# Decay rows in four loads on three queues, fillers on another bank, and the first half of w_in ahead of x0, in a state-space and GELU kernel

## The chip, the cores and the metric

The kernel runs on one core of a Trainium2 chip. A core has five engines that run their own instruction streams and meet at semaphores: TensorE (PE, matmuls, with a separate row PEld for loading weights), VectorE (DVE), ScalarE (ACT), GpSimd (POOL) and SyncE (SP). Data move between the chip's main memory (HBM), the on-chip SBUF and, by the engines alone, the matmul accumulators (PSUM, in banks of 128 x 512 fp32). Transfers are done by 16 DMA engines; SP, ACT and POOL each have a queue from which they issue them. The metric is the time of one execution on the device in microseconds; the median over several executions is compared.

## The reference

Two stages. The first is a state-space layer over 4 batches, 8 heads, 768 positions, head size 32 and state size 16, worked in chunks. In each chunk, with `cum` the running sum of the log of the clipped decays `a`:

```
L = exp(cum_i - cum_j), i >= j;   M = (C B^T) * L
y = M x  +  (C state) * exp(cum)
state = exp(sum) * state + sum_j B_j x_j exp(cum_end - cum_j)
```

The second takes `y` as 3072 tokens of 256 features, and computes `g = gelu_tanh(y w_in)` with 2048 hidden features, and `out = g w_out`. Inputs and output are fp32.

## The kernel before

The chunk is 128 positions, so a batch has 6 chunks and there are 24 in all. They are grouped in units: chunk 0, chunk 1, and then pairs, 13 units.

**Decay.** The decays of all 32 (batch, head) rows are loaded into one tile `a_t` of 128 x 256: four groups of 32 partitions, group q holding positions 192 q onward. Its first 192 columns come by one load on SP (line 153) and the other 64, for three groups, by one load on ACT (line 155); the rest is set to one by DVE (line 142). DVE clips it (`f_clip`, line 268), runs a product scan with restarts at chunk ends (`f_R`, 272), transposes the result in 32 x 32 blocks into `rt` (`f_RT`, 277) and takes reciprocals (`f_recip`, 281). C is scaled with the one and B with the other (`f_mul`, line 311), both to bf16. So the factor exp(cum_i - cum_j) sits in the operands, and M needs only the causal mask.

**One batch.** The scaled C and B are transposed by PE (`f_T`, 322) into PSUM and copied to SBUF as `ce` (C, in two copies with alternate heads zeroed by `par`) and `bh` (B); `f_N` (357) transposes `bh` back per chunk to `bn`. Batch 0 has its own split version of these steps (`sequence0`), in which B's transposes go to the bank `yb` and C's to `o_ps`; the copy of B is done by DVE for the first two chunks (257) and by ACT for the rest (253).

**One unit.** `f_G` (390): eight Gram matmuls per chunk pair into the four banks `gb`. `f_M` (400): DVE multiplies by the causal mask `tri`. `f_D` (411): the state's increment B^T x into a bank `hp`. `f_S` and `f_SP` (459, 461, 468): DVE updates the state and spreads it with `bmask`. `f_Y` (433, 442): PE adds the chunk's own part and the state's part into `yb`. `f_yev` (451): ACT copies the result to `xm`, transposed as the next stage wants it. x is cast to bf16 by POOL (255) ahead of that.

**Second stage.** `f_s1` (492): w_in times `xm` into `hp` or, for some groups of unit 0, `o_ps`; `f_gelu` (500) on ACT; `f_s2` (509): w_out; `f_oev` (516, 518) copies the result out and `f_store` (522) has SP issue the store. w_in comes in two halves of 1 MB (`load_wi`, 244) and w_out in four quarters (`load_wo`, 249); POOL casts them, and ACT half of the first quarter of w_in.

**The order.** All engines' programs are fixed when the kernel is built. Each step is a node with an engine, an estimated duration, its dependencies and a priority; `run_order` (line 31) simulates the engines with these estimates, picks at each time the node of the best priority that is ready, and writes the instructions in that order. Loads are nodes of a DMA engine with a duration and a delay `done` until they can be used; SP issues them in the order in which the nodes are made:

```
an = load(TD + 0.3, none)
load_bc_n(0, 1, 0)
load_x_n(0)
load_w_n(0)
load_x_n(1)
load_w_n(1)
```

Where PE would be idle early on by the planner's clock, `idle` (736) puts in filler matmuls on a tile of zeros `wz` (line 744), which write columns 384 to 511 of `yb` and are read by nobody. There are 69 of them, in blocks of 44, 7, 10, 6, 1 and 1. The number in a block is worked out from the length of the planner's gap. Every DMA has one of eight completion semaphores in turn, and a DMA whose semaphore has been used waits at its issuing engine until the earlier user is complete. The second pair of w_out quarters waits in addition until POOL has done the last w_in cast.

Of the kernel before, what the change touches and what calls it, by code (L numbers as in the profile page):

```python
# [93 lines left out]
def kernel(  # L94
# [10 lines left out]
    nc = tc.nc  # L105

    batch, H, S, D = x.shape
    N = B.shape[-1]
    Q = 128
# [3 lines left out]
    QS = S // 4  # L113
# [25 lines left out]


    a_t = const.tile([128, 2 * Q], FP32, name="a_t")
    nc.vector.memset(a_t[96:128, QS:], 1.0)
    XF, X16 = {}, {}
    U = [dict() for _ in range(batch)]

    def load_bc(b, i):
# [3 lines left out]
        nc.sync.dma_start(out=d["bc"][:, i],  # L150
                          in_=(B, C)[i][b].rearrange("h (p r) n -> p h (r n)", r=R6))

    nc.sync.dma_start(out=a_t[:, 0:QS], in_=bass.AP(
        tensor=a.tensor, offset=a.offset, ap=[[QS, 4], [S, batch * H], [1, QS]]))
    nc.scalar.dma_start(out=a_t[0:96, QS:], in_=bass.AP(
        tensor=a.tensor, offset=a.offset + QS,
        ap=[[QS, 3], [S, batch * H], [1, 2 * Q - QS]]))

    wz = const.tile([128, 512], BF16, name="wz")
    nc.vector.memset(wz, 0.0)  # L160
    warm = const.tile([128, 1], FP32, name="warm")
# [45 lines left out]
    for e in range(2):  # L207
        nc.vector.tensor_reduce(out=par[:, e:e + 1],
                                in_=bmp[:, e, :, 0:1].rearrange("p g o -> p (g o)"),
# [12 lines left out]
    gb = ps1.tile([128, 4, 512], FP32, name="gb")  # L222
    yb = ps1.tile([128, 512], FP32, name="yb")
# [252 lines left out]
    def third(u, i):  # L476
        return u < 1 and (4 * u + i) % 3 == 0
# [51 lines left out]
    def add(eng, dur, fn, *args, deps=(), prio=0.0, done=None):  # L529
        n = Node(eng, dur, (lambda: fn(*args)), deps, prio,  # L530
                 (0.26 if eng == "PE" else 0.0) if done is None else done)
        n.name = f"{fn.__name__}{args}"
        nodes.append(n)
        return n
# [7 lines left out]
    def load(dur, fn, *args, deps=()):  # L542
        nload[0] += 1
        return add("DMA", dur, fn, *args, deps=deps, done=0.9, prio=nload[0])
# [3 lines left out]
    Gn, Mn, Dn, Yn, yevn, Sn, SPn = ({} for _ in range(7))  # L548
    cen, bhn, bnn = {}, {}, {}

    an = load(TD + 0.3, none)

    def load_bc_n(b, *which):
        for i in which:
            bl[(b, i)] = load(1.6, load_bc, b, i)

    def load_x_n(*us):
        for u in us:
            xl[u] = load(0.87 * len(UNITS[u]), load_x, u)

    def load_w_n(*qs, o=False):
        for q in qs:
            if o:
                won_l[q] = load(1.5, load_wo, q)
            else:
                win_l[q] = load(2.5, load_wi, q)

    load_bc_n(0, 1, 0)
    load_x_n(0)
    load_w_n(0)  # L570
    load_x_n(1)
    load_w_n(1)
    load_x_n(2)
    load_w_n(0, 1, 2, 3, o=True)
# [14 lines left out]

    cl = add("DVE", 0.35, f_clip, deps=[an], prio=-90)  # L590
    R_ = add("DVE", 0.68, f_R, deps=[cl], prio=-89)
    RT_ = add("DVE", 0.27, f_RT, deps=[R_], prio=-88)
    rc1 = add("DVE", 0.46, f_recip, 0, 1, deps=[RT_], prio=-62)
    pen = add("DVE", 0.32, f_pe, deps=[R_], prio=-19)
    mul_c = add("DVE", 0.97, f_mul, 0, 1, deps=[bl[(0, 1)], rc1], prio=-61)
    mul_b = add("DVE", 0.97, f_mul, 0, 0, deps=[bl[(0, 0)], RT_], prio=-60)
    rc2 = add("DVE", 1.35, f_recip, 1, batch, deps=[RT_], prio=45)
    ppn = add("PE", 0.4, f_pp, deps=[pen], prio=-28)
    pendn = add("ACT", 0.2, f_pend, deps=[ppn], prio=-29)
    ppn.takes("hp", pendn)  # L600

    PB = 1000.0
    gpn, geln, oevn = {}, {}, {}

# [19 lines left out]
    def sequence0():  # L624

        t1 = add("PE", 0.34, f_T, 0, 1, deps=[mul_c], prio=-70)
        t0 = add("PE", 0.34, f_T, 0, 0, deps=[mul_b, t1], prio=-69)
        fa = [add("ACT", 0.4, f_F0, e, "ACT", 0, PA, deps=[t1], prio=-70) for e in range(2)]
        ea = add("DVE", 0.36, f_E, 0, 0, "DVE", 0, PA, deps=[t0], prio=-70)
        na = add("PE", 0.12, f_N, 0, 0, 2, deps=[ea], prio=-25)  # L630
        ba = add("ACT", 0.3, f_bn, 0, "ACT", 0, 2, deps=[na], prio=-20)
        fb = [add("ACT", 0.55, f_F0, 0, "ACT", PA, 128, deps=[t1], prio=-18),
              add("ACT", 0.55, f_F0, 1, "ACT", PA, 128, deps=[t1], prio=-17)]
        eb = add("ACT", 0.55, f_E, 0, 0, "ACT", PA, 128, deps=[t0], prio=-47)
        nb = add("PE", 0.24, f_N, 0, 2, CPB, deps=[eb, na], prio=-24)
        bb = add("ACT", 0.4, f_bn, 0, "ACT", 2, CPB, deps=[nb], prio=-19)
        t1.takes("o", *fa, *fb)
        t0.takes("yb", ea, eb)
        na.takes("hp", ba, bb)
        for c in range(CPB):  # L640
            cen[c], bhn[c], bnn[c] = (fa, ea, ba) if c < 2 else (fa + fb, eb, bb)


    for u, cs in enumerate(UNITS):
        n = len(cs)
        q = 10.0 * cs[0]
        e = "POOL"
        xcn[u] = add(e, 0.42 if n == 1 else 0.62, f_castx, u, e, deps=[xl[u], Yn.get(u - 5)], prio=q - 12)
        if u == 0:
            sequence0()  # L650
# [14 lines left out]
        for k in range(n):  # L665
# [3 lines left out]
            else:  # L669
                ms.append(add("DVE", 1.24, f_M, u, k, 0, 4, deps=[gn] + ms,  # L670
                              prio=q + 1 + 0.1 * k if u > 1 else -16 + 2 * u + 0.1 * k))
# [5 lines left out]
        for k, gc in enumerate(cs):  # L677
            if gc % CPB == CPB - 1:
# [4 lines left out]
                          prio=q + 1.5 + 0.1 * k if u > 1 else -13.5 + u)  # L683
        Dn[u].takes("hp", *ss)
        deps = ms + [xcn[u]] + [SPn[c - 1] for c in cs if c % CPB > 0]
# [11 lines left out]
    for u, cs in enumerate(UNITS):  # L697
        n = len(cs)
        c0 = cs[0]
        per = 512 // (n * Q)  # L700
        for i in range(4 * n):
            f_last = (i * per + per - 1) // 4
            gpn[(u, i)] = add("PE", 0.437, f_s1, u, i,
                              deps=[yevn[u]] + wi_n[f_last] + ([gpn[(u, i - 1)]] if i else [gpn.get((u - 1, 4 * len(UNITS[u - 1]) - 1))] if u > 2 else []),
                              prio=PB + 10 * c0)
            geln[(u, i)] = add("ACT", 0.57, f_gelu, u, i, deps=[gpn[(u, i)]], prio=PB + 10 * c0 + i)
            gpn[(u, i)].takes("o" if third(u, i) else "hp", geln[(u, i)])
    prev = None
    s2_first = []
    for u, cs in enumerate(UNITS):  # L710
        n = len(cs)
        per = 512 // (n * Q)
        for tt, gc in enumerate(cs):
            pool = "yb" if gc >= NCH - TAIL and gc % 2 == 0 else "o"
            oeng = "DVE" if gc >= NCH - TAIL and gc % 2 else "ACT"
            for q in range(4):
                need = [geln[(u, i)] for i in range(4 * n) if i * per <= 4 * q + 3]
                nd = add("PE", 0.437, f_s2, u, tt, q, pool, deps=need[-1:] + [wo_n[q], prev],
                         prio=PB + 45 + 10 * cs[0] + tt)
                if q == 0:  # L720
# [15 lines left out]
    def idle(t0, t1):  # L736
        t0 = max(t0, 1.25)
        n = int((t1 - t0 - 0.05) / (0.107 if t0 < 6.3 else 0.2 if 9.5 < t0 < 13.2 else 0.07))
        if gpn[(0, 0)].start is not None or n < 1:
            return None  # L740

        def fill():
            for _ in range(n):
                nc.tensor.matmul(out=yb[:, 384:512], lhsT=wz[:, 0:128], rhs=wz[:, 0:128],  # L744
                                 start=True, stop=True)
        return fill

    pools = {"hp": 2, "o": 1, "gram": 2, "yb": 1, "wf": 4, "ob": 6}
    for t, fn in run_order(nodes, pools, idle=idle, wait=("DVE", "POOL")):
        fn()  # L750
# [30 lines left out]
```

## Time and profile before

| | us |
|---|---|
| median of 13 executions | 124.94 (124.44 to 125.89) |
| profiled execution | 124.93 |
| its span, first to last instruction | 123.2 |
| PE busy | 111.4 (90%) |
| ACT busy | 75.2 (61%) |
| DVE busy | 63.3 (51%) |
| POOL busy | 19.7 (16%) |
| clip of the decays starts | 5.66 |
| first transposes (batch 0, C) start | 8.77 |
| first Gram products start | 13.52 |
| first w_in matmuls start | 17.30 |
| transposes of batch 1 start (C, B) | 30.52, 32.96 |

The span is what the profile covers; the 1.73 us between it and the execution's time lie before the first and after the last instruction. Times in the profile count from the start of the span. A view by timeline gives for each group of instructions its start, length, engine, source line, operation, and in brackets how long the engine had been idle and what released it. The chain of work that ended last is followed back from the last instruction; it names a DMA where a transfer was the last thing waited for, and SPq where SP's queue of DMA issues was. A view by windows gives the busy time of each engine in a stretch, the clock that was granted to TensorE (1.00 is full, 0.5 half), the mean busy share of the 16 DMA engines (over 1 where records of transfers overlap) and the bytes moved per second. Over the whole span the granted clock is 0.972; it is low between 9 and 16 us.

### The profile page before, as it was taken

Reading aid. Unit: us, or ns where it says so; the run is one execution under the profiler, and the core shown is the slowest. Engines: PE = TensorE matmul, PEld = TensorE weight load, DVE = VectorE, ACT = ScalarE, POOL = GpSimd, SP = SyncE. Lnnn points to the kernel's source line nnn. Section 1 sums busy time; section 2 is a strip of 40 time slices with the busy share of each in tenths; the row PEclk is TensorE's granted clock in tenths of the full one; section 3 lists DMA queues with packets and bytes.
Section 4 is the critical chain, followed back from the end, with each engine's and each line's share of the span. In section 5 each row is a group of like instructions: output and inputs, shape, how many; then the busy total and the mean of one; then the engine's idle time right before and its main releaser. Section 6 shows DMA issues by size and latency. Waiting matters only on the chain.

```text
span 123.2 us, 3421 instructions
## 1 busy us (share of the span) xinstructions
PE 111.4 (90%) x1471; PEld 94.5 (77%) x1471; DVE 63.3 (51%) x112; ACT 75.2 (61%) x145; POOL 19.7 (16%) x37
## 2 busy tenths in 40 slices
PE   5916987998699999999999999999999999999980
PEld 5915756785597788797878888787878888888870
DVE  5193399874837998753959618292936000000100
ACT  2206359574395676579667688656677778666410
POOL 7310666750211123121000000000000000000000
PEclk9995599999999999999999999999999999999999
DMA  0989998999959989980111010011110110011121
GB/s 16 250 203 243 367 213 249 337 211 170 167 103 286 170 143 284 169 150 11 37 43 43 5 43 20 28 43 43 48 43 0 48 43 21 24 48 43 43 85 43
DMA packets 39637, 13.96 MB, mean 113 GB/s; under 512 B 33863, under 2 KB 39111, under 8 KB 39623
## 3 DMA queue, kind: packets, MB, share of 16 engines
q1 hardware_dynamic: 39524, 13.73, 48.5%
q8 instruction: 11, 0.18, 0.7%
q10 hardware_dynamic: 99, 0.02, 0.1%
q14 instruction: 3, 0.02, 0.1%
HBM read 10.61 MB, written 3.15 MB: 112 GB/s over the span
## 4 chain that ended last, share of the span: by engine, by line
PE 70%; DMA 13%; SPq 8%; DVE 4%; POOL 2%; issue 1%; DVEq 0%
PE o_ps L509 29%; PE hp L492 29%; DMA wf<-in_moe_w_in_dram 8%; DMA bc_t<-in_C_dram 6%; SPq L236 4%; PE yb L509 3%; PE gb L390 2%; PE yb L433 2%; PE yb L442 2%; POOL w_in_sb L255 2%; PE gb L322 2%; DVE ch L257 1%; DVE bc L311 1%; SPq L244 1%; SPq L150 1%; PE gb L357 1%
## 5 line engine op out<-in xcount | busy, mean ns | idle before, releaser
L500 ACT ACTIVATE gT<-hp 128x512 bf16<-128x512 f32 x94 | 52.2, 596 | 20.1 <-PE hp L492 19.8
L492 PE MATMUL hp<-xm,w_in_sb 128*128 128x256 bf16 (+1 forms) x400 | 50.7, 266 | 0.3 <-ACT xm L451 0.2
L509 PE MATMUL o_ps<-w_out_sb,gT 128*128 128x256 bf16 x352 | 47.3, 273 | 0.0
L492 PEld LDWEIGHTS <-w_in_sb 128*128 128x128 bf16 x416 | 37.2, 98 | 5.8 <-issue 1.8
L509 PEld LDWEIGHTS <-gT 128*128 128x128 bf16 x384 | 37.1, 98 | 4.8 <-issue 0.4
L400 DVE TENSOR_TENSOR m<-gb,tri 128x1024 bf16<-128x1024 f32 (+1 forms) x25 | 29.0, 1174 | 2.6 <-PE gb L390 2.5
L518 DVE COPY o_sb<-o_ps 128x256 f32<-128x256 f32 x2 | 0.8, 424 | 25.1 <-PE o_ps L509 25.1
L255 POOL CAST x<-x_t 128x512 bf16<-128x512 f32 (+1 forms) x13 | 8.3, 639 | 29.5 <-DMA x_t<-in_x_dram 18.9
L468 DVE SCALAR_TENSOR_TENSOR sp_new<-s_new,pend,bmask 128x256 bf16<-128x256 f32 x20 | 11.0, 553 | 0.2
L744 PE MATMUL yb<-wz 128*128 128x128 bf16 x69 | 8.2, 305 | 2.6 <-DVE warm L162 1.4
L516 ACT ACTIVATE o_sb<-o_ps 128x256 f32<-128x256 f32 x20 | 7.7, 384 | 4.4 <-ACT gT L500 2.7
L461 DVE SCALAR_TENSOR_TENSOR s_new<-s_new,pend,hp 128x64 f32<-128x64 f32 x16 | 4.5, 280 | 10.3 <-PE hp L411 9.9
L744 PEld LDWEIGHTS <-wz 128*128 128x128 bf16 x69 | 7.3, 147 | 3.0 <-issue 1.5
L451 ACT ACTIVATE xm<-yb 128x512 bf16<-128x512 f32 (+1 forms) x13 | 7.4, 567 | 3.3 <-PE hp L411 3.0
L322 PEld LDWEIGHTS <-bc 128*128 128x128 bf16 x48 | 3.4, 104 | 5.3 <-DVE bc L311 4.0
L442 PE MATMUL yb<-m,x 128*32 128x128 bf16 x192 | 6.2, 220 | 0.0
L390 PE MATMUL gb<-ce,bh 32*128 32x256 bf16 x96 | 5.0, 283 | 1.1 <-DVE m L400 1.1
L339 ACT ACTIVATE ce<-o_ps,par 128x258 bf16<-128x258 bf16 (+1 forms) x4 | 2.2, 582 | 5.5 <-PE o_ps L322 5.5
L433 PE MATMUL yb<-ce,sp_new 128*32 128x128 bf16 x160 | 5.3, 221 | 0.0
L459 DVE COPY s_new<-hp 128x64 f32<-128x64 f32 x4 | 0.9, 222 | 8.5 <-PE hp L411 8.5
L311 DVE TENSOR_TENSOR bc<-bc_t,pt 128x768 bf16<-128x768 f32 x4 | 3.8, 954 | 2.5 <-DMA bc_t<-in_C_dram 2.5
L255 POOL CAST w_in_sb<-wf 128x1024 bf16<-128x1024 f32 (+1 forms) x4 | 3.8, 981 | 5.6 <-DMA wf<-in_moe_w_in_dram 5.6
(59 smaller groups left out, 61.4 us busy)
## 6 DMA issues: line engine op xcount, KB each, us to landing
x_t<-in_x_dram SPq DMA_DIRECT2D x24, 128.0 KB, 4.6
out_dram<-o_sb SPq DMA_DIRECT2D x24, 128.0 KB, 1.7
wf<-in_moe_w_in_dram SPq DMA_DIRECT2D x2, 1024.0 KB, 8.5
wf<-in_moe_w_out_dram SPq DMA_DIRECT2D x4, 512.0 KB, 5.8
bc_t<-in_C_dram SPq DMA_DIRECT2D x4, 384.0 KB, 4.7
bc_t<-in_B_dram SPq DMA_DIRECT2D x4, 384.0 KB, 4.6
a_t<-in_a_dram SPq DMA_DIRECT2D x1, 96.0 KB
a_t<-in_a_dram ACTq DMA_DIRECT2D x1, 24.0 KB
```

Source lines behind the costliest of these rows:

```text
L255: nc.gpsimd.tensor_copy(out=o, in_=i)
L390: nc.tensor.matmul(out=gb[:, g, 256 * k:256 * k + 256], lhsT=bh_of(gc)[32 * g:32 * g + 32], rhs=ce_of(gc)[32 * g:32 * g + 32], start=True, ...
L400: nc.vector.tensor_tensor(out=MT[gc][:, g0:g1], in0=gb[:, g0:g1, 256 * (k + half(u)):256 * (k + half(u)) + 256] .rearrange("p g (e t) -> p ...
L433: nc.tensor.matmul(out=y4[32 * j:32 * j + 32, k, w], lhsT=sp[:, 32 * h:32 * h + 32], rhs=ce_of(gc)[:, h % 2], start=first(j), stop=False, ...
L442: nc.tensor.matmul(out=y4[32 * j:32 * j + 32, k, w], lhsT=X16[u][:, k, 32 * h:32 * h + 32], rhs=m[:, h // 2, h % 2, :], start=first(j), st ...
L451: nc.scalar.activation(xm[:, :, t0:t0 + n * Q].rearrange("p w (c t) -> p c w t", c=n), y4[:, 0:n], AF.Copy)
L468: nc.vector.scalar_tensor_tensor(out=sp_new.rearrange("p (g d) -> p g d", g=4), in0=state[("s", gc)].rearrange("p (o d) -> p o d", o=1).to ...
L492: nc.tensor.matmul(out=hp[:, j * nt:(j + 1) * nt], lhsT=w_in_sb[:, kc, fi * 128:(fi + 1) * 128], rhs=xm[:, kc, t0:t0 + nt], start=(kc == 0 ...
L500: nc.scalar.activation(gts[u][:, i * per:(i + 1) * per, 0:nt], hps.pop((u, i)).rearrange("p (j t) -> p j t", j=per), AF.Gelu_apprx_tanh)
L509: nc.tensor.matmul(out=ops[gc], lhsT=gts[u][:, fi, tt * Q:(tt + 1) * Q], rhs=w_out_sb[:, fi, :], start=(fi == 0), stop=(fi == NF - 1), ski ...
L516: nc.scalar.activation(o_sb, ops.pop(gc), AF.Copy)
L744: nc.tensor.matmul(out=yb[:, 384:512], lhsT=wz[:, 0:128], rhs=wz[:, 0:128], start=True, stop=True)
```

## The change

Four things.

1. The decay tile is loaded by four DMAs, one for each group of 32 partitions: group 0 (256 columns) on SP, group 1 (192) and group 2 (256) on ACT, group 3 (192) on POOL. The columns beyond 192 of groups 1 and 3 are set to one. Each load is now a plain pattern of 32 rows on both sides, where the two before had 4 x 32 and 3 x 32 rows of memory on one side.
2. SP issues the first half of w_in directly after batch 0's C and B; x of unit 0 and of unit 1 follow it, and then the second half of w_in.
3. Fillers that the planner places between the transposes of batch 0's B and the first Gram products write to the fourth bank of `gb` and not to `yb`, which ACT and DVE read at that time.
4. The planner is told a later use of the decays (delay 1.3 instead of 0.9) and a longer block transpose (0.53 instead of 0.27).

```diff
-    nc.vector.memset(a_t[96:128, QS:], 1.0)
+    for q in (1, 3):
+        nc.vector.memset(a_t[32 * q:32 * q + 32, QS:], 1.0)
...
-    nc.sync.dma_start(out=a_t[:, 0:QS], in_=bass.AP(
-        tensor=a.tensor, offset=a.offset, ap=[[QS, 4], [S, batch * H], [1, QS]]))
-    nc.scalar.dma_start(out=a_t[0:96, QS:], in_=bass.AP(
-        tensor=a.tensor, offset=a.offset + QS,
-        ap=[[QS, 3], [S, batch * H], [1, 2 * Q - QS]]))
-
+    for q, eng in enumerate((nc.sync, nc.scalar, nc.scalar, nc.gpsimd)):
+        n = QS if q % 2 else 2 * Q
+        eng.dma_start(out=a_t[32 * q:32 * q + 32, 0:n], in_=bass.AP(
+            tensor=a.tensor, offset=a.offset + q * QS, ap=[[S, batch * H], [1, n]]))
...
     an = load(TD + 0.3, none)
+    an.done = 1.3
...
     load_bc_n(0, 1, 0)
-    load_x_n(0)
     load_w_n(0)
-    load_x_n(1)
+    load_x_n(0, 1)
     load_w_n(1)
...
-    RT_ = add("DVE", 0.27, f_RT, deps=[R_], prio=-88)
+    RT_ = add("DVE", 0.53, f_RT, deps=[R_], prio=-88)
...
+    T0n = []
...
         t0 = add("PE", 0.34, f_T, 0, 0, deps=[mul_b, t1], prio=-69)
+        T0n.append(t0)
...
+        g_next = T0n[0].start is not None and Gn[0].start is None
+
         def fill():
             for _ in range(n):
-                nc.tensor.matmul(out=yb[:, 384:512], lhsT=wz[:, 0:128], rhs=wz[:, 0:128],
+                nc.tensor.matmul(out=(gb[:, 3] if g_next else yb)[:, 384:512], lhsT=wz[:, 0:128], rhs=wz[:, 0:128],
                                  start=True, stop=True)
```

The written order follows the planner's new estimates. In the built program the fillers are 68, in blocks of 51, 8, 4 and 5. On PE the matmul `f_pp` (293), which spreads the chunk-end decays, now stands behind the transposes of B; the state increments of units 0 and 1 stand together behind the first `f_Y`; and the w_in and w_out groups from 19.8 to 33 us of the old profile are interleaved a little differently, with the same work ahead of each transpose of batch 1. On DVE the product for B of batch 0 comes ahead of `f_pe`, one `f_SP` and one `f_S` change places with their neighbours, and the state update `f_S` ahead of batch 1's first product stands before it and not after. On ACT the copy `f_pend` stands two copies later. On POOL the load of decay group 3 is ahead of all set-up, and the casts of w_in's first half are ahead of those of x0 and x1. On SP the semaphores of the decay loads are the ones that the second half of w_in and the two x loads of unit 2 wait for.

## The prediction

> **What bounds the kernel now.** I read the page's slices first, then the chain that ended last, then the opening by timeline and by windows. TensorE (PE) is busy 90% of the 123.2 us span and nearly without a gap from 33 us on, so what can be won lies ahead of that. The chain (start us, length us, what):
>
> ```profile
> 7.31 9.26 DMA wf<-in_moe_w_in_dram
> 16.57 0.05 issue
> 16.62 2.23 POOL w_in_sb L255 x2
> ...
> 22.15 7.26 DMA bc_t<-in_C_dram
> ...
> 29.50 0.96 DVE bc L311
> 30.46 0.20 DVE s_new L461
> ...
> 31.17 0.87 DVE bc L311
> 32.04 0.88 DVE ch L257
> ...
> 32.96 0.49 PE gb L322 x6
> ```
>
> To see: the chain does not run through the decay rows or the first chunks. It runs down SP's queue: second half of w_in landed at 16.57, cast by POOL until 18.85, then the issues behind it, then C of batch 1 landed at 29.41, DVE's two products and a copy, and the second transposes at 32.96. After them PE is almost all of the chain. So the end moves by what these transposes move, if PE arrives in time.
>
> The opening by timeline (start, length, engine, what, idle before and releaser):
>
> ```profile
> 0.79 1.52 ACTq L155 DMA_DIRECT2D a_t<-in_a_dram  x1
> 2.79 2.46 SPq L236 DMA_DIRECT2D x_t<-in_x_dram  x1
> 5.66 0.29 DVE L268 TENSOR_SCALAR ac<-a_t 128x256 f32<-128x256 f32 x1 [2.74 <-DMA a_t<-in_a_dram]
> 10.38 0.85 PE L322 MATMUL yb<-ident,bc 128*128 128x128 bf16 x6
> 12.37 1.22 PE L744 MATMUL yb<-wz 128*128 128x128 bf16 x10 [1.14 <-ACT bh L253]
> 13.52 0.61 PE L390 MATMUL gb<-ce,bh 32*128 32x256 bf16 x8
> 17.30 0.62 PE L492 MATMUL o_ps<-xm,w_in_sb 128*128 128x128 bf16 x8
> 29.31 0.60 PE L509 MATMUL o_ps<-w_out_sb,gT 128*128 128x256 bf16 x4
> 30.52 0.51 PE L322 MATMUL gb<-ident,bc 128*128 128x128 bf16 x6 [0.60 <-DVE bc L311]
> ```
>
> To see: ten fillers wait 1.14 us for ACT to leave their bank, then hold the first Gram products (L390) until 13.52. PE reaches batch 1's transposes at 29.92 and waits 0.60 and, before 32.96, 0.94 us.
>
> Windows of the loads (second number the length; last three: granted clock, DMA share, GB/s):
>
> ```profile
> 6.50:7.00 0.50, 0.00 (x0) 0.00 (x0) 0.47 (x2) 0.00 (x0) 0.00 (x0) 1.00 0.98 171
> 7.00:8.00 1.00, 0.00 (x0) 0.00 (x0) 0.93 (x3) 0.00 (x0) 0.00 (x0) 1.00 0.82 135
> 8.00:9.00 1.00, 0.23 (x4) 0.23 (x5) 0.90 (x3) 0.00 (x0) 0.27 (x1) 1.00 0.88 283
> ```
>
> To see: a hole at 7 to 8 us, while w_in's first half, issued behind x0, has hardly begun. Two lines on queues (packets, MB, share):
>
> ```profile
> q8 instruction: 11, 0.18, 0.7%
> q10 hardware_dynamic: 99, 0.02, 0.1%
> ```
>
> ACT's 99 packets are its 96 rows and three completions: three engines did that load. In the trace's packet records 12 of C's 16 completions come by 4.79 us, four at 5.54 to 5.86, so SP's decay load sat on four engines and put them about 0.8 us (5.54 less 4.79, to 1.07 at most) behind.
>
> **The change, part by part.**
>
> *Decay rows.* Four loads of 32 rows, one on SP, two on ACT, one on POOL, in place of two. ACT's second issue ends between 0.79 + 2 x 0.42 = 1.63 (SP's shortest issue row) and 0.79 + 2 x 1.52 = 3.83. Add 0.75 (SP's decay issue ended at 1.50, its first packet is at 2.25) and 0.93 (last ACT packet 4.73, clip 5.66): 3.3 to 5.5. POOL's load has no row: between the same 3.3 and 0.79 + 9.3 = 10.1, the longest issue-to-landing of the page; I take 0.79 + 4.6, the median of the 128 KB x loads, so 4.9 with the small size in mind. Clip then starts at 4.9, 0.76 earlier; batch 0's C, complete at 5.86, is there for the product at 7.0. POOL's set-up goes behind its issue: bmask ends at 2.66 and par, on DVE ahead of the clip, at 2.93. There are 2.0 us of room before 4.9, so an issue like ACT's 1.52 stays hidden; one of 3 us would cost 1.0 here. The second memset of a_t is 0.11 us in DVE's 2.74 us idle. ACT's second issue is ahead of the table load (2.35 to 3.63), used first at 9.37: hidden.
>
> *Fillers and DVE order.* Fillers are 51, 8, 4, 5 instead of 44, 7, 10, 6, 1, 1. The seven more in the first block lie in the 2.72 us that PE waits before 8.77. In DVE's order batch 0's B product now precedes the two small pe operations (8.63 to 9.08), so it is 0.45 earlier; one filler more (0.11) takes some back, and the pp matmul (0.45 to the next start) leaves PE's path ahead of the B transposes: these gain 0.35. From their start to L390 was 3.14 us (10.38 to 13.52). Now: 0.85, pp 0.45, four unblocked fillers at 0.115 each (1.15 between starts / 10), 1.76; DVE's copy, 0.43 after the 0.85, fits within. Gain 1.4. Bounds: 0 if another reader of gb held the fillers, 1.8 if only DVE's copy counts. pend goes behind bh on ACT; its first user is at 16.85: hidden.
>
> So L390 comes 0.76 + 0.35 + 1.4 = 2.5 earlier, at 11.0, and L492 would start near 14.8. Its casts: see next.
>
> *w_in ahead of x0.* SP's x0 issue (2.46) and w_in's (1.47) change places, and x1 follows x0. The bytes ahead of w_in's second half are the same. What it gains: the hole, (283 - 135)/283 x 1.0 = 0.52 plus 0.14 in the half microsecond before (171 against 237 GB/s earlier), 0.66. The even decay loads give the four late engines 0.8. It may be that the one caused the other (SP waits for room on the latest engine), so 0.7 to 1.5 together; below, 0 if those engines catch up in any case. The other way: an instruction fetch (q8: 0.7% of 16 x 123.2 us / 11 = 1.25 us each) begins at 16.25, just behind the last w_in packet at 15.89; it follows PE's progress and would now fall into that transfer, 0 to 1.25, taken as 0.4. Landing 16.57 - 1.4 + 0.4 = 15.6, POOL done at 17.8 instead of 18.85. The x0 and x1 casts (0.40 each) stand ahead of these on POOL, in its 1.60 us wait. x0, cast at 8.73 before, now lands behind 1 MB: near 12.5; Y0 needs it with the second mask product, about 13.3. Hidden, with 0.8 of cover.
> New waits on SP: w_in's second half and both x2 loads wait for decay semaphores, done by 5 us when SP gets there after 7; behind them stand all later loads.
>
> *What reaches the end.* PE: the group that needs the last w_in cast was at 19.81, now at 17.9, so it could reach batch 1's transposes at 28.0. C of batch 1: the queue ahead gains 1.4, and the w_out issue gated by POOL gains 1.0; I take 1.2, so 28.2, and the transposes 29.3. s_new (0.20) goes ahead of the product in DVE's order, so the second transposes gain 1.4, and with 0.1 kept back for a cold first group the end gains 1.3. PE's order after that is nearly unchanged, and the 0.97 stall at 68.24 stays.
>
> Sum: 124.93 (profiled execution: 123.2 and 1.73 around it, at the median of 124.94) - 1.3 = 123.6.
>
> **Two rules weighed.** ACT's 99 packets came first. The Trainium skill, "DMA: Bandwidth & Descriptors", on why a DMA increments its semaphore by 16, says that a load runs on the largest number up to 16 that divides the slowest dimensions of both sides: 4, then 3 here, and 16 after. By that the four engines lose their lag wholly, 1.5 in place of 1.4, end 123.5. Its rules for kernel authors speak against the change: spreading loads over issuing engines buys only issue time, and loads of disjoint partitions share the same engines. By that rule alone only the hole counts, 0.66, end 124.3.
>
> **Rivals.**
> 1. *Hidden anyway.* One late engine sets C's landing: in the packet records 15 of its completions are in by 27.6, the last near 29.2, and a fetch runs at 25.5 on some engine. If fetches, not the decay rows, made it late, C lands as before and PE merely waits longer at 30.52. For: the fetch lies on C's transfer. Against: the lag is there at 5.5 us, before any fetch. Gain 0.2 from s_new: 124.7.
> 2. *Slower: POOL's row lands late.* From clip to L492 was 11.64, now 11.64 - 1.75 = 9.9. L492 had 12.62 to the transposes at 29.92; later than 17.9 it delays them even against before, so the turning point is a landing at 8.0. At 10.1, L492 is at 20.0, 2.1 past that; 0.9 is absorbed in the wait before 32.96: +1.2, 126.1. Against: only 24 KB. The skill's same page gives loads from GpSimd about 1 us to the first byte and 2 us fixed; by that the landing is an estimated 3.8 and the sum stays.
> 3. *PE still cold.* The clock is 0.51 from 9 to 14. Eight up-projection matmuls start 0.45 apart warm; at half clock six such groups cost 6 x 0.45 = 2.7, less 1.3 of waiting to spare: +0.1 over before, 125.0 to 125.7 if the fetch delays w_in too.
>
> **How the numbers follow.** A measurement tells 0.3% (0.37 us) from no change. Forecast 0.58, own range 122.7 to 124.4; hidden 0.20, a quarter of it faster; POOL late 0.12; cold 0.10, a third each way about no change. Faster 0.58 + 0.05 + 0.01 = 0.64, same 0.15 + 0.04 = 0.19, slower 0.12 + 0.05 = 0.17. The range goes to 122.6 (both bounds of the transfers) and 125.4 (into the slower cases).
>
> **What would show it.** Clip near 4.9; L390 at about 11 without a wait for ACT; no hole at 7 to 8 us; w_in's second half landed near 15.6; C of batch 1 near 28.2; second transposes near 31.6. Wrong if a POOL load sits ahead of the clip, or C stays at 29.4.

## The result, and the profile after

The changed kernel takes 123.63 us (median of 11 executions, 122.62 to 124.16) against 124.94: a ratio of 0.988, with a 95% interval of 0.9852 to 0.9908 (the two medians alone give 0.9895). Ratios here and below leave out executions that are more than 1.5% above the fastest of their kernel. The forecast was 123.6. The profiled execution took 123.84 us, with a span of 122.1.

The chain of waits up to batch 1's second transposes, after (start, length, what):

```profile
5.22 10.09 DMA wf<-in_moe_w_in_dram
...
15.36 2.04 POOL w_in_sb L254 x2
...
21.34 2.81 SPq L151
...
24.18 5.41 DMA bc_t<-in_B_dram
...
29.61 0.96 DVE bc L310
30.57 0.88 DVE ch L256
...
31.49 0.49 PE gb L321 x6
```

It is the chain of before, down SP's queue, with one difference: the load of batch 1 that DVE waits for last is B, not C. Line numbers are one lower than before. The second transposes start at 31.49 instead of 32.96, 1.47 earlier, and nothing after them gives that back: the last copy of the output, released by PE, starts at 118.39 instead of 119.86, again 1.47. The last store then takes longer, 3.7 us to the end of the span against 3.3, so that the span shrinks by 1.1 and the median by 1.31.

The opening and batch 1's transposes by timeline, after:

```profile
1.32 0.65 POOL L156 DMA_DIRECT2D a_t<-in_a_dram  x1 [0.81 <-POOLq L768]
3.26 1.92 SPq L235 DMA_DIRECT2D x_t<-in_x_dram  x2
4.73 0.29 DVE L267 TENSOR_SCALAR ac<-a_t 128x256 f32<-128x256 f32 x1 [0.61 <-DMA a_t<-in_a_dram]
8.72 0.51 PE L321 MATMUL yb<-ident,bc 128*128 128x128 bf16 x6
9.32 0.38 PE L747 MATMUL gb<-wz 128*128 128x128 bf16 x4
9.75 0.40 PE L389 MATMUL gb<-ce,bh 32*128 32x256 bf16 x8
11.95 0.29 PE L441 MATMUL yb<-m,x 128*32 128x128 bf16 x8 [0.90 <-POOL x L254]
13.22 1.03 PE L491 MATMUL o_ps<-xm,w_in_sb 128*128 128x128 bf16 x8
29.26 0.50 PE L321 MATMUL gb<-ident,bc 128*128 128x128 bf16 x6
31.49 0.49 PE L321 MATMUL gb<-ident,bc 128*128 128x128 bf16 x6 [0.63 <-DVE ch L256]
```

The clip starts 0.93 earlier, the first Gram products 3.77 earlier and without a wait for ACT, the first w_in matmuls 4.08 earlier. The first transposes of batch 1 gain only 1.26, so most of the 4 us has been lost on the way. The same view shows where, in the waits of PE between them:

```profile
16.46 1.07 PE L491 MATMUL hp<-xm,w_in_sb 128*128 128x128 bf16 x16 [0.81 <-POOL w_in_sb L254]
18.79 0.24 PE L410 MATMUL hp<-x,bn 128*32 128x64 bf16 x8 [0.27 <-POOL x L254]
22.13 0.60 PE L508 MATMUL o_ps<-w_out_sb,gT 128*128 128x256 bf16 x4 [0.34 <-POOL w_out_sb L254]
24.00 0.60 PE L508 MATMUL o_ps<-w_out_sb,gT 128*128 128x256 bf16 x4 [0.40 <-POOL w_out_sb L254]
27.36 0.21 PE L410 MATMUL hp<-x,bn 128*32 128x64 bf16 x4 [0.67 <-ACT gT L499]
```

PE has come early to weights that are not there yet. From the first w_in matmuls to the first transposes it takes 16.04 us (29.26 less 13.22) where it took 13.22 (30.52 less 17.30). Of the 2.82 more, 1.36 is waiting: the five waits above sum to 2.49 and one of 0.19 stands between them, against 0.56, 0.16 and 0.60 before. The rest, 1.46, is about what the half clock of the next view would take (half of its 2.98 us of PE, an estimate).

Windows of after (length, busy time of PE, PEld, DVE, ACT and POOL, granted clock, DMA share, GB/s):

```profile
7.00:8.00 1.00, 0.15 (x3) 0.15 (x4) 1.00 (x2) 0.00 (x0) 0.00 (x0) 1.00 0.98 366
9.00:10.00 1.00, 0.96 (x19) 0.62 (x15) 0.45 (x2) 1.00 (x3) 0.04 (x1) 1.00 0.86 121
10.00:11.00 1.00, 0.99 (x19) 0.62 (x11) 0.81 (x2) 1.00 (x4) 1.00 (x2) 1.00 0.69 98
12.50:16.00 3.50, 2.98 (x41) 2.12 (x40) 3.36 (x7) 1.63 (x4) 0.64 (x1) 0.51 1.00 235
```

The hole at 7 to 8 us is filled (366 GB/s against 135), but a new one lies at 9 to 11. And the half clock, which before lay between 9 and 16 us, now lies at 12.5 to 16, on the first w_in groups.

### The profile page after: what moved, and what is told of

Read it like the earlier page. It is cut to its first block, busy times and chain, and to the rows that moved or that the text cites. A ratio compares the mean times of both kernels' runs of the same rounds, so it can differ in the third digit from the quotient of the medians.

```text
span 122.1 us, 3425 instructions
## 1 busy us (share of the span) xinstructions
PE 110.6 (91%) x1470; PEld 93.4 (77%) x1470; DVE 62.9 (51%) x113; ACT 75.0 (61%) x145; POOL 19.9 (16%) x38
## 4 chain that ended last, share of the span: by engine, by line
PE 70%; DMA 13%; SPq 9%; DVE 3%; POOL 2%; issue 1%; DVEq 0%
PE o_ps L508 30%; PE hp L491 28%; DMA wf<-in_moe_w_in_dram 8%; DMA bc_t<-in_B_dram 4%; SPq L235 4%; SPq L151 3%; PE yb L508 3%; PE gb L389 2%; PE yb L441 2%; PE yb L432 2%; PE gb L321 2%; POOL w_in_sb L254 2%; DVE ch L256 2%; PE gb L356 1%; DVE bc L310 1%; SPq L243 1%
## 5 line engine op out<-in xcount | busy, mean ns | idle before, releaser
L491 PEld LDWEIGHTS <-w_in_sb 128*128 128x128 bf16 x416 | 37.8, 100 | 6.9 <-issue 1.9
L460 DVE SCALAR_TENSOR_TENSOR s_new<-s_new,pend,hp 128x64 f32<-128x64 f32 x16 | 4.5, 280 | 15.8 <-PE hp L410 15.3
L254 POOL CAST x<-x_t 128x512 bf16<-128x512 f32 (+1 forms) x13 | 7.5, 581 | 25.5 <-DMA x_t<-in_x_dram 21.0
L467 DVE SCALAR_TENSOR_TENSOR sp_new<-s_new,pend,bmask 128x256 bf16<-128x256 f32 x20 | 10.1, 512 | 0.0
L747 PE MATMUL yb<-wz 128*128 128x128 bf16 x64 | 6.0, 276 | 1.6 <-DVE warm L161 1.6
L747 PEld LDWEIGHTS <-wz 128*128 128x128 bf16 x68 | 5.9, 129 | 1.6 <-DVE warm L161 1.6
L441 PEld LDWEIGHTS <-x 128*32 128x32 bf16 x192 | 3.8, 99 | 1.7 <-POOL x L254 1.1
```

Source lines behind the costliest of these rows:

```text
L254: nc.gpsimd.tensor_copy(out=o, in_=i)
L441: nc.tensor.matmul(out=y4[32 * j:32 * j + 32, k, w], lhsT=X16[u][:, k, 32 * h:32 * h + 32], rhs=m[:, h // 2, h % 2, :], start=first(j), st ...
L467: nc.vector.scalar_tensor_tensor(out=sp_new.rearrange("p (g d) -> p g d", g=4), in0=state[("s", gc)].rearrange("p (o d) -> p o d", o=1).to ...
L491: nc.tensor.matmul(out=hp[:, j * nt:(j + 1) * nt], lhsT=w_in_sb[:, kc, fi * 128:(fi + 1) * 128], rhs=xm[:, kc, t0:t0 + nt], start=(kc == 0 ...
L747: nc.tensor.matmul(out=(gb[:, 3] if g_next else yb)[:, 384:512], lhsT=wz[:, 0:128], rhs=wz[:, 0:128], start=True, stop=True)
```

## The experiments

The reasons were tested by making each part alone and by undoing each part. In the expectations, A is the prediction's account, in which the loads and the order share the gain; B is its rival, in which PE's earlier start makes it; D was formed after the first four runs and gives the whole gain to the decay loads. Ratios are to the kernel before, on the same chip, with 95% intervals. Executions of one kernel spread by about 1% either way, so that variants 0.3% apart are not told apart here. Milestones are from one profiled execution each, which can lie up to 1.1 us from the kernel's median.

### The four decay loads alone

```diff
-    nc.sync.dma_start(out=a_t[:, 0:QS], ...)
-    nc.scalar.dma_start(out=a_t[0:96, QS:], ...)
+    for q, eng in enumerate((nc.sync, nc.scalar, nc.scalar, nc.gpsimd)):
...
```

> The kernel before with the four decay loads alone; order of w_in and x0, fillers and planner numbers as before. Theory A (the end is set by when C and B of batch 1 have landed, and even decay loads remove the lag of four DMA engines): clip near 4.7 instead of 5.66, completions of the first C all within 0.6 us of each other, w_in's second half landed near 15.8 instead of 16.57, second transposes of batch 1 0.7 to 1.0 us earlier than 32.96, time 124.1 (ratio 0.993). Theory B (the end follows the start of the second stage on TensorE, which the fillers held): the first w_in matmuls move with the clip, 0.9 us, and the time is 124.1 as well if the chain is TensorE's, but then the wait ahead of 32.96 stays at 0.9 us. Theory C (the loads are hidden): 124.9.

Measured: 123.61 us, 0.9865 (0.9816 to 0.9914), the whole gain of the full change. SP's issues of this kernel by timeline, and a window of it:

```profile
2.33 0.92 SPq L235 DMA_DIRECT2D x_t<-in_x_dram  x1
3.29 1.45 SPq L243 DMA_DIRECT2D wf<-in_moe_w_in_dram  x1
4.78 0.47 SPq L235 DMA_DIRECT2D x_t<-in_x_dram  x1
5.30 1.09 SPq L243 DMA_DIRECT2D wf<-in_moe_w_in_dram  x1
```

```profile
7.00:8.00 1.00, 0.00 (x0) 0.00 (x0) 0.97 (x2) 0.00 (x0) 0.56 (x1) 1.00 1.00 373
```

The issue of x0 takes 0.92 us in place of 2.46, and starts 0.46 earlier, so SP is two microseconds ahead of before from there on: the second half of w_in is issued at 5.30 (7.31 before) and its cast starts at 14.59 (16.62). The hole at 7 to 8 us is gone although x0 still stands ahead of w_in. By the trace's packet records batch 0's C completes on all 16 engines between 3.97 and 4.48, where four engines came at 5.54 to 5.86 before. So the late engines and a long issue on SP go together, and with the issue goes all that follows. It is so in every run: behind C and B of batch 0 the next issue takes 2.46 to 2.82 us in the four kernels with the old loads and 0.60 to 1.57 in the ten with even ones. That SP waits there for the late engines is the likely reading; no view shows that wait by itself.

What bounds this kernel is then something else. Its chain of waits runs from the decay rows through PE, ACT and DVE, with no load of the second stage in it:

```profile
1.32 3.57 DMA a_t<-in_a_dram
...
28.38 0.48 DVE sp_new L467
28.86 0.87 DVE bc L310
29.73 0.88 DVE ch L256
...
30.65 0.49 PE gb L321 x6
...
44.16 1.28 DVE bc L310
45.45 0.88 DVE ch L256
...
46.37 0.49 PE gb L321 x6
```

The transposes of batch 1 are at 28.82 and 30.65, earlier than in the full change, but at batch 2's PE waits 0.74 us for DVE. The last copy starts at 118.37, as in the full change (118.39).

### w_in first, alone

```diff
     load_bc_n(0, 1, 0)
-    load_x_n(0)
     load_w_n(0)
-    load_x_n(1)
+    load_x_n(0, 1)
     load_w_n(1)
```

> The kernel before with the first half of w_in ahead of x0 alone. Theory A: the hole at 7 to 8 us fills, w_in's second half lands 0.4 to 0.7 us earlier, the second transposes of batch 1 0.4 to 0.7 us earlier, time 124.4 (ratio 0.996). Theory B: the first w_in matmuls do not move, since their casts were not what they waited for, time 124.9. If the hole came from the four late engines, it stays, and the time is 124.9 also.

Measured: 124.57 us, 0.9942 (0.9911 to 0.9974). SP's issue behind C and B is as long as before (w_in's, 2.52 us): it is long whatever stands there. Windows of this kernel:

```profile
7.00:8.00 1.00, 0.00 (x0) 0.00 (x0) 0.93 (x3) 0.00 (x0) 0.00 (x0) 1.00 0.97 294
10.00:11.00 1.00, 1.00 (x12) 1.00 (x10) 0.03 (x1) 1.00 (x4) 0.00 (x0) 0.50 1.27 204
11.00:12.00 1.00, 0.42 (x4) 0.26 (x3) 0.43 (x1) 0.29 (x2) 0.94 (x2) 0.50 1.19 165
```

The hole moves to 10 to 12 us. The packet records name it: x comes in packets of 128 bytes, 1871 of which end in these two microseconds, and 26 of w_in's 4096. What is gained at 7 to 8 us is given back where x0 and x1 now stand one behind the other, and the second half of w_in is cast at 16.45, only 0.17 earlier than before. The 0.6% comes later: C of batch 1, issued at 22.17 as before (22.15), is there for its product at 28.55 instead of 29.50, and the second transposes start at 32.07. Why its transfer was shorter was not settled; this profiled execution, 124.03, was also the fastest of its twelve.

### Fillers and the planner's order, alone

```diff
     an = load(TD + 0.3, none)
+    an.done = 1.3
...
-    RT_ = add("DVE", 0.27, f_RT, deps=[R_], prio=-88)
+    RT_ = add("DVE", 0.53, f_RT, deps=[R_], prio=-88)
...
-                nc.tensor.matmul(out=yb[:, 384:512], ...)
+                nc.tensor.matmul(out=(gb[:, 3] if g_next else yb)[:, 384:512], ...)
```

> The kernel before with the fillers on gb's fourth bank and the two planner numbers (and so the new order on PE and DVE); both decay loads and the order of w_in and x0 as before. Theory A: first Gram products about 1.7 us earlier than 13.52, TensorE waits longer ahead of batch 1's transposes, these move by 0 to 0.2 us, time 124.8 (ratio 0.999). Theory B: the end follows the first w_in matmuls, 1 to 1.5 us earlier, time 123.7 (ratio 0.990).

Measured: 124.98 us, 0.9974 (0.9942 to 1.0006). The first Gram products start at 11.09 and the first w_in matmuls at 15.71, 1.6 earlier than before, yet batch 1's transposes only 0.47 and 0.30, with this wait:

```profile
32.66 0.49 PE L322 MATMUL gb<-ident,bc 128*128 128x128 bf16 x6 [1.00 <-DVE ch L257]
```

B falls: PE's earlier start by itself is spent on waiting for the loads, which are unchanged (126 GB/s at 7 to 8 us).

### Each part undone in the full change

The old decay loads put back:

```diff
-    for q, eng in enumerate((nc.sync, nc.scalar, nc.scalar, nc.gpsimd)):
...
+    nc.sync.dma_start(out=a_t[:, 0:QS], ...)
+    nc.scalar.dma_start(out=a_t[0:96, QS:], ...)
```

> The changed kernel with the two decay loads of before (w_in first, fillers and planner numbers as changed). Theory D: the four late engines are back, first completions of C spread over 1.4 us, and the time is that of w_in first alone, 124.2 to 124.6 (ratio 0.992 to 0.997), since TensorE waits for batch 1 in both. If the parts add up, w_in first and the fillers together give 0.9916: 123.9.

Measured: 124.65 us, 0.9958 (0.9923 to 0.9992); the profiled execution was 1.1 us above the median, so its times late in the kernel are not compared. Without the loads two thirds of the gain are gone.

The order of x0 and w_in put back:

```diff
     load_bc_n(0, 1, 0)
+    load_x_n(0)
     load_w_n(0)
-    load_x_n(0, 1)
+    load_x_n(1)
     load_w_n(1)
```

> The changed kernel with x0 back ahead of w_in's first half (decay loads, fillers and planner numbers as changed). Theory D (the even decay loads alone make the gain, and w_in first adds nothing beside them): w_in's second half lands near 14.6, C of batch 1 near 26.6, second transposes of batch 1 at 29.5 to 30.7; time 123.0 to 123.7 (ratio to before 0.984 to 0.990), with a wait for DVE before 47 us taking back what is gained beyond the changed kernel. Theory A as first put (order and loads each have a share, 0.66 and 0.8 us): 124.2 (0.994).

Measured: 123.79 us, 0.9869 (0.983 to 0.9908). Nothing is lost. The second half of w_in is cast 0.29 earlier than in the full change, at 15.07, but the second transposes start at 31.53 (31.49) and not at the 29.5 to 30.7 expected: DVE waits 0.69 us for B.

The fillers put back on `yb`:

```diff
-                nc.tensor.matmul(out=(gb[:, 3] if g_next else yb)[:, 384:512], ...)
+                nc.tensor.matmul(out=yb[:, 384:512], ...)
```

> The changed kernel with all fillers on yb, all orders as changed. First Gram products 0.5 to 1.2 us later than 9.75, since four fillers wait for ACT and DVE to leave yb. Theory A and D: TensorE has 3 us of waits ahead of batch 1's second transposes, so these and the time stay: 123.6 (0.9895). Theory B (end follows the second stage's start): 124.2 to 124.8.

Measured: 124.01 us, 0.9893 (0.9846 to 0.9939). The first Gram products are 0.97 later, at 10.72; the second transposes of batch 1 are not later, at 31.29. A loss of 0.1% can't be told from none.

### Where POOL's row decides

Its load issued behind POOL's set-up instead of ahead of it:

```diff
-    for q, eng in enumerate((nc.sync, nc.scalar, nc.scalar, nc.gpsimd)):
+    def a_row(q, eng):
...
+    for q, eng in enumerate((nc.sync, nc.scalar, nc.scalar)):
+        a_row(q, eng)
...
+    a_row(3, nc.gpsimd)
```

> The changed kernel with POOL's decay load moved behind POOL's set-up, so that it is issued near 5 us instead of 1.3. The clip then starts near 7.7 instead of 4.73, the first w_in matmuls near 16.2 instead of 13.2. If the prediction's turning point holds (a landing at 8.0 us, before which TensorE still reaches batch 1's transposes in time) the time is 123.6 to 124.0; if the end follows the clip, 126.5.

Measured: 127.52 us, 1.0172 (1.0133 to 1.0211), slower than before. The load and the clip by timeline, and the chain:

```profile
4.34 0.64 POOL L156 DMA_DIRECT2D a_t<-in_a_dram  x1
10.62 0.61 DVE L271 TENSOR_SCALAR ac<-a_t 128x256 f32<-128x256 f32 x1 [7.59 <-DMA a_t<-in_a_dram]
```

```profile
4.34 6.25 DMA a_t<-in_a_dram
10.62 0.62 DVE ac L271
...
33.33 0.87 DVE bc L314
34.20 0.88 DVE ch L260
35.12 0.50 PE gb L325 x6
```

The expected clip was 7.7; the size was wrong by 2.9 us, since a load issued 3.0 us later landed 5.9 later. The mechanism of the prediction's second rival is there. The prediction set the turning point at a landing of 8.0, with the first w_in matmuls 9.9 behind the clip and the transposes 12.62 behind these. By that they would be at 20.5 and 33.1; they are at 21.23 and 33.10. Its price, 2.6 (20.5 less 17.9) less 0.9 of waiting that is absorbed, would be 1.7 for this landing. The second transposes are at 35.12, 2.16 later than before, with 0.42 of the wait left; the time is 2.28 above.

The same row on SP:

```diff
-    for q, eng in enumerate((nc.sync, nc.scalar, nc.scalar, nc.gpsimd)):
+    for q, eng in enumerate((nc.sync, nc.scalar, nc.scalar, nc.sync)):
```

> The changed kernel with the fourth decay load on SP in place of POOL, behind the first. POOL's load was the last of the four (packets to 4.0 us, clip 4.73); without it the clip waits for ACT's second load and starts at 4.0 to 4.2, while C and B go out 0.4 us later. Theory D (TensorE waits for batch 1's B in any case): second transposes at 31.2 to 31.9, time 123.4 to 124.0 (ratio 0.986 to 0.992). If the end follows the clip, 122.9.

Measured: 124.28 us, 0.9921 (0.9889 to 0.9953). The clip is at 3.52, 1.21 earlier than in the full change, and the time is not better. SP's extra issue of 0.47 puts all its later loads back: B of batch 1 is there for its product at 30.29 instead of 29.61, and PE waits 1.36 us for the second transposes, which start at 32.17, later than the 31.2 to 31.9 expected. So the clip is off the chain once it is early enough, and SP's queue is on it.

All four rows on SP, in the kernel before:

```diff
-    nc.sync.dma_start(out=a_t[:, 0:QS], ...)
-    nc.scalar.dma_start(out=a_t[0:96, QS:], ...)
+    for q, eng in enumerate((nc.sync, nc.sync, nc.sync, nc.sync)):
...
```

> The kernel before with the four decay loads of 32 rows all issued by SP, one after the other; nothing on ACT or POOL, everything else as before. C goes out about 0.8 us later than before. If what counts is that each load is spread evenly over the DMA engines (theory D), the first C's completions stay within 0.6 us of each other, and w_in's second half lands at 15.0 to 15.8 instead of 16.57: time 123.7 to 124.4 (ratio 0.987 to 0.993). If it is the three queues, nothing is gained: 124.9 to 125.7.

Measured: a ratio of 0.9924 (0.9878 to 0.997), from six of the twelve executions; by the medians of all, 124.79 against 125.27, it is 0.996. The four issues take 1.78 us on SP, and C is issued at 2.62 (1.56 before, 1.25 in the loads alone). C's completions all come between 4.98 and 5.52, none late, and x0's issue takes 0.60: the even pattern alone does away with the late engines and the long issue. But the profiled execution (124.87) shows little gain from it:

```profile
16.98 2.02 POOL L254 CAST w_in_sb<-wf 128x1024 bf16<-128x1024 f32 x2 [2.90 <-DMA wf<-in_moe_w_in_dram]
32.77 0.49 PE L321 MATMUL gb<-ident,bc 128*128 128x128 bf16 x6 [0.94 <-DVE ch L256]
```

The second half of w_in, issued 0.98 earlier than before, at 6.33, was expected at 15.0 to 15.8 and is there for its cast at 16.98 (16.62 before); the second transposes are 0.19 earlier than before. The first half of w_in is cast 0.94 earlier than before, at 12.14, but by the packet records the second half's packets then end over 4.85 us (11.60 to 16.45), where they took 3.54 (12.35 to 15.89); why was not settled. So how much of the gain the even pattern keeps without the other two queues is open: by the two ratios 0.8% or 0.4%, of the 1.35% of the loads alone.

### Is there more behind it?

A fourth buffer for the weights (and two fewer for x), so that the second pair of w_out quarters need not wait until POOL has cast w_in:

```diff
-    wfp = ctx.enter_context(tc.tile_pool(name="wfp", bufs=3))
-    ldx = ctx.enter_context(tc.tile_pool(name="ldx", bufs=NU))
+    wfp = ctx.enter_context(tc.tile_pool(name="wfp", bufs=4))
+    ldx = ctx.enter_context(tc.tile_pool(name="ldx", bufs=NU - 2))
```

> The changed kernel with a fourth buffer for the weights' fp32 tiles (and two buffers fewer for x), so that the third w_out quarter no longer waits until POOL has cast w_in; all instruction orders the same. If the queue behind that wait sets when C and B of batch 1 land (theory A), the DMA share of 0.82 to 0.86 at 17 to 20.5 us rises, they land 0.3 to 0.8 us earlier than 28.0 and 29.6, time 123.1 (ratio to before 0.985). If the 16 engines are full anyway, or TensorE has become the limit, 123.6 (0.9895).

Measured: 123.75 us, 0.9871 (0.9823 to 0.9919). SP issues the third quarter at 17.03 instead of 17.42, and the DMA share from 17 to 20.5 us is 0.91 instead of 0.84, but B's product is not earlier, at 29.68 (29.61). The granted clock stayed full in its profile (0.998 over the span), and the second transposes still start at 31.56, behind a wait of 1.09. So the half clock of after costs nothing there: what it takes is waited for otherwise (PE waits 2.29 us for w_in's cast, where it waits 0.81 in the full change).

B and C of batch 1 issued ahead of unit 3's x, in the full change:

```diff
     load_w_n(0, 1, 2, 3, o=True)
+    load_bc_n(1, 1, 0)
     load_x_n(3)
     for b in range(1, batch):
-        load_bc_n(b, 1, 0)
+        if b > 1:
+            load_bc_n(b, 1, 0)
```

> The changed kernel with C and B of batch 1 ahead of unit 3's two x loads on SP (and the planner's order that follows). Theory D: B lands 1 to 2 us earlier than 29.59, the second transposes at 29.5 to 30.5, time 122.6 to 123.2 (ratio 0.980 to 0.986). If the floor is DVE's work between batch 1 and 2 (a wait of TensorE for DVE near 46 us grows by what is won) or unit 3's x is now late, 123.6.

Measured: 123.55 us, 0.9868 (0.982 to 0.9915). B's product starts at 28.54 and the second transposes at 30.42, 1.07 earlier than in the full change, and the time does not follow. The trace shows why: the planner's order has changed with the loads. After these transposes PE still has 1164 matmuls and 88.08 us of work before the last copy, where the full change has 1124 and 86.63, so that the microsecond is taken up by work that stood ahead of them.

The same with the decay loads alone:

```diff
     load_w_n(0, 1, 2, 3, o=True)
+    load_bc_n(1, 1, 0)
     load_x_n(3)
...
```

> The kernel with the decay loads alone and C and B of batch 1 ahead of unit 3's x loads. In the run with the loads alone TensorE was late for batch 1's transposes and waited only 0.33 us there and 0.74 at 46 us, so earlier C and B should give little: 123.4 to 123.8 (ratio 0.985 to 0.989). If C and B were still the limit, 122.9.

Measured: a ratio of 0.9909 (0.9868 to 0.995), above the 0.985 to 0.989 expected and not better than the loads alone. Here 1168 matmuls stand behind the second transposes, which start at 30.57. So no kernel whose second transposes come about a microsecond ahead of the full change's (30.65, 30.42 and 30.57) is faster than it: with the loads alone the wait of 0.74 at 46.37 takes most of the microsecond, and with B and C first PE's order does. No kernel was found that clearly beats the change.

## Why the prediction was right

| step | predicted | after |
|---|---|---|
| clip starts | 4.9 | 4.73 |
| first Gram products | 11.0 | 9.75 |
| first w_in matmuls | 14.8 | 13.22 |
| second half of w_in landed | 15.6 | 15.31 |
| POOL done with it | 17.8 | 17.4 |
| first transposes of batch 1 | 29.3 | 29.26 |
| second | 31.6 | 31.49 |
| gain at the second transposes | 1.4 | 1.47 |
| time | 123.6 | 123.63 |

**Right: what the end hangs on.** The chain was read as SP's queue, then batch 1's products and second transposes, then PE to the end. The transposes moved by 1.47 and the last copy by 1.47. The other runs bear this out: in all twelve kernels where the same 1124 matmuls follow the second transposes, the last copy starts 86.9 us after them, but for the loads alone (87.7, with the wait of 0.74) and the fillers on `yb` (87.3, with a wait of 0.37 at 46.60). Where other work follows them, as with B and C first, the end does not move with them. The first rival, that batch 1's loads land as before, falls: the product for C starts at 28.05 (29.50 before), that for B at 29.61 (31.09). One name is off: the prediction followed C, and B is the one that lands last, 0.20 us after DVE was ready for it.

**Right: the clip, with POOL's row as the last.** The profile of after lists the loads of `a_t` (the last number is the time in us from issue to landing):

```profile
a_t<-in_a_dram SPq DMA_DIRECT2D x1, 32.0 KB, 1.6
a_t<-in_a_dram ACTq DMA_DIRECT2D x1, 32.0 KB, 2.5
a_t<-in_a_dram ACTq DMA_DIRECT2D x1, 24.0 KB, 1.8
a_t<-in_a_dram POOLq DMA_DIRECT2D x1, 24.0 KB, 3.4
```

POOL's is issued at 1.32 and takes 3.4 us, so it lands at 4.7, within the bounds of 3.3 and 10.1 and close to the choice of 4.9, which was a guess between wide bounds; the prediction's other estimate, 3.8, was 0.9 too early. The landing stands 3.3 us ahead of the rival's turning point of 8.0. The late row, landing at 10.6, shows a loss of that kind, 2.16 at the second transposes where the rival's sum gives 1.7; where the turning point lies was not measured.

**Too small: PE's gain up to the first Gram products.** The fillers and DVE's order were put at 1.4 and 0.35. From B's transposes to the Gram products it is now 1.03 (9.75 less 8.72) and was 3.14, so 2.1; from C's transposes to B's 0.87 and was 1.61, so 0.74. The durations had been taken from rows at half clock. Now this stretch runs at full clock, with the same six transposes in 0.51 us where they took 0.85, and a filler in 0.10 for 0.115. None of this reached the end.

**Wrong: the cover of x0.** It was to land near 12.5, with 0.8 us to spare. By the packet records its data were there at about 9 us, and yet PE waited 0.90 us for its cast at 11.95. POOL was the reason: the two casts of w_in's first half, 9.96 to 11.55, now stand ahead of the cast of x0. The step counted the transfer that x0 was moved behind and not the casts, on the other queue that it was moved behind. The wait cost nothing, since PE had to wait for w_in's second half after it.

**Wrong: what is worth what.** The prediction gave 1.4 us to the transfers, 0.66 of it from the hole and 0.8 from the four late engines, less 0.4, and noted that the one may have caused the other. The runs show that these are not two terms. The loads alone fill the hole and bring the cast of the second half 2.03 us forward, to 14.59. In the full change it is at 15.36: 0.48 is lost with the fillers and the planner's order (15.07 with only x0's order undone), and the new order of x0 another 0.29, because the hole has only moved to 9 to 11 us, where x comes in packets of 128 bytes. Of these two only the order's part is seen in more than one pair of runs: w_in's last packet comes at 13.90, 14.29 and 14.40 in the three kernels with even loads on three queues and x0 first, and at 14.81 to 15.59 in the six with w_in first. The 14.40 is the loads alone with B and C of batch 1 first, without the planner's order, so the 0.48 may be no more than the spread between executions. The transfer of the second half takes 10.09 us there, and 9.48 with the order undone. The 0.4 for an instruction fetch was misplaced: by the packet records the fetch begins at 15.04, behind the last packet of w_in at 14.87, as it did before, at 16.25 behind 15.89; nor did it follow PE, whose first w_in matmuls came 4.08 earlier and the fetch 1.21. So a net gain of 1.0 was predicted and 1.26 measured, from 2.03 for the loads where 0.8 stood, and a loss where the order was to gain 0.66. That the sum came out within 0.03 us of the median is luck in part: a term far too small, one of the wrong sign and one for a fetch that fell elsewhere nearly cancelled. In the chances, the shares of the third rival (0.01, 0.04 and 0.05) are not the thirds that the sentence names; with thirds the three sums would be 0.66, 0.18 and 0.15.

**The rule on engines.** The packet records show the four late engines, and that they vanish when each load has 32 rows. The Trainium skill, "DMA: Bandwidth & Descriptors", in the section on why a DMA increments its semaphore by 16, says that a load runs on the largest number of engines up to 16 that divides the slowest dimensions of both its sides; the 4 and 3 of the old patterns fit it. The rule of the same page, in its rules for kernel authors, that splitting by partitions or over issuing engines brings no bandwidth, would by the prediction's reading have had this change gain only the hole, for an end of 124.3. The loads alone decide against that reading here (0.9865), and putting the old ones back takes two thirds of the gain (0.9958). How the gain divides between the even pattern and the issue time that the other queues save, which the same rule does grant, is open (0.9924 or 0.996 with all four on SP).

**Still open.** In the full change, with x0's order undone, and with a fourth weight buffer, B of batch 1 gates the second transposes at 31.5; with the loads alone it does not, and w_out's last packet arrives at 22.57 instead of 23.83. What in the order of the planner delays w_out there was not settled, nor why the second half of w_in takes longer with all four decay rows on SP.

## What to carry to other kernels

A small load whose slowest dimension is 3 or 4 can delay everything behind it: here the old decay loads ran on three and four DMA engines, these were late for the next load, and the issue behind took 2.5 to 2.8 us. Four even loads on three queues were worth 1.3% of the kernel. Look for completions of one transfer that come in two groups, and for an issue that takes microseconds. When several edits aim at the same wait, run each alone, because their gains do not add; before a milestone is compared between kernels, see that the same work stands behind it; and when a load is moved, count the queue of the engine that casts it as well.

## What the runs showed of the hardware

- A load issued by POOL lands 3.4 us after its issue begins when it is issued at 1.32, and 6.3 us after when it is issued at 4.34, with the weights in flight. By the packet records its first packet comes 1.6 and 3.5 us after the end of the issue.
- Two plain loads of 32 rows take ACT 0.90 us to issue together; one load of 96 rows in a pattern of three dimensions took 1.52.
- A transfer in 128-byte packets leaves a trough: 121 and 98 GB/s from 9 to 11 us, where 968 of the 977 data packets that end have 128 bytes, against 366 at 7 to 8 us, where 89 of 102 have 4096.
- The clip and the product scan took 0.61 and 1.40 us on DVE in the late-row kernel, while POOL cast w_in (10.48 to 12.13) and then x; they take 0.29 and 0.69 in after, where POOL does its set-up at that time.
